# A depthwise conv and an ELU MLP on one core: two conv taps move from TensorE to VectorE, and the last piece of x is loaded early

## The chip, the cores and the metric

The kernel runs on one core of a Trainium2 chip. The metric is the device time in microseconds of one execution, here as the median of several. TensorE, VectorE (DVE), ScalarE (ACT), GpSimd (POOL) and the sync engine (SP) each run their own instruction stream in order, and wait for each other through semaphores.

## The reference

The input x is 8 x 4096 tokens of 192 values, that is 32768 rows. Each of 8 heads has 24 of the 192 columns and 7 weights. The weights go through a softmax, and each head's columns are convolved along the sequence with them (causally, zeros before the sequence). Then follow a matmul to 2048 columns, an ELU, and a matmul back to 192.

```python
w = np.exp(w - max(w)); w = w / (sum(w) + 1e-09)          # (8 heads, 7 taps)
out = np.einsum('hk,bskhg->bshg', w, x_unf)                # conv along s, 24 columns per head
h = out.reshape(B * S, D) @ w_in                           # (32768, 192) @ (192, 2048)
g = np.where(h > 0.0, h, np.exp(np.minimum(h, 0.0)) - 1.0)
return g @ w_out                                           # (2048, 192)
```

## The kernel before

The 32768 tokens are cut into 32 tiles of 1024 tokens (`NS`, index s). One half of a tile lies on partitions 0 to 63 of the h matmuls' operands and the other on 64 to 127, so two matmuls of 64 rows run side by side on TensorE. For each tile and each of 16 blocks of 128 hidden columns (`n` counts these blocks over all tiles, 512 in all) and each half, one *unit* runs: three h matmuls (L962) add up a 128x512 block of h in a PSUM bank; ScalarE makes exp(h) (L727); GpSimd clamps it to at most 1 (L684); VectorE makes max(exp - 1, h) and writes it as `gT` (L823), which frees the bank; the o matmuls (L985) use `gT` and `w_out`. There are eight PSUM banks. ScalarE also copies the conv's result (L723) and the outputs (L737) out of PSUM.

The order of TensorE's matmuls is written by a planner in the kernel's head (`pe_order`). It is a fixed list: every engine follows its own part of it, whatever the times turn out to be. The planner's costs and lists are not touched by the change.

The conv of tiles 1 to 31 is a matmul with a band matrix. `wband` holds each head's 7 weights in a row of zeros; SP writes it to DRAM (`conv_band`) with a row pitch one larger than the row, and reads it back as `Tm`, so that the weights lie on diagonals. The windows of x for it come by GpSimd's own DMAs (`load_x`, L600), which convert fp32 to bf16 on the way, two per tile. The last tile's second half has its fifth window, 70 rows, in a DMA of its own, because a full window would reach past the end of x. Their places in GpSimd's stream are in `x_before`.

The conv of tile 0 does not wait for the band. x is loaded as fp32 (`xs`), cast by ScalarE (`xb`), transposed by TensorE (`t` items, L884 and L895), and copied to `xT`, one 512-column row for each of three chunks j of 64 channels in two halves. Then TensorE multiplies `xT`, shifted by the tap, with `taps`, diagonal matrices of the weights (`d` items, L911): 7 matmuls of 512 columns for chunks 0 and 1, and 14 of 256 columns for chunk 2. ScalarE and VectorE copy the sums to `att` (L718, L809, L811), and the first h matmuls start. Before that VectorE also makes `taps` (L785), and copies two column parts of `w_in` from partitions 0 to 63 to 64 to 127 (`upper_half`, L748); ScalarE copies a third at its place `COPY_AT` (L733), and an SP DMA the rest (L1024). GpSimd meanwhile issues all start-up loads of `w_in`, `w_out` and x.

`first_read` says how many of ScalarE's (`s_fa`) and VectorE's (`s_fd`) start-up copies must be done before a start-up bank has been read.

Of the kernel before, what the change touches and what calls it, by code (L numbers as in the profile page):

```python
# [38 lines left out]
WCOLS = ((0, 4 * FC), (4 * FC, 8 * FC), (8 * FC, 16 * FC))  # L39
WOUT = (0, 4, 8, 16)  # L40
HALO = 8
BW = P + CW
XI = SUP // P
MM_H, MM_O, MM_C = 216.0, 82.5, 102.5
AHEAD = 100.0
# [18 lines left out]
def bass_lightweight_conv__then__act_elu_kernel(  # L64
# [327 lines left out]
    def tt_count(n, r):  # L392
        return unit_at[n, r] + 1

    band = nc.dram_tensor("conv_band", (P, HEADS * BW + P), BF16).ap()

    with ExitStack() as stack:
        def sbuf(name, shape, dt):
            return stack.enter_context(nc.sbuf_tensor(name, shape, dt))
# [4 lines left out]
        def sema(name):  # L404
            return stack.enter_context(nc.semaphore(name))
# [23 lines left out]
        wsum = sbuf("wsum", [HEADS, 1], FP32)  # L429
        wrs = sbuf("wrs", [HEADS, 1], FP32)  # L430
        wn = sbuf("wn", [HEADS, KSIZE], BF16)
        wnb = sbuf("wnb", [HEADS, HEADS, KSIZE], BF16)
        owner = sbuf("owner", [HEADS, P], BF16)
        block8 = sbuf("block8", [HEADS, HEADS, KSIZE], BF16)
        wband = sbuf("wband", [P, HEADS, BW], BF16)
        zw = sbuf("zw", [P, GS], BF16)
        scr = sbuf("scr", [P, 2], FP32)
        H = psum("H", [P, NBANK, GS])
# [28 lines left out]
        s_wd = sema("s_wd")  # L467
        s_wa = sema("s_wa")
        s_band = sema("s_band")
        s_att = [sema(f"s_att{i}") for i in range(2)]  # L470
        s_od = sema("s_od")
        s_cswap = sema("s_cswap")
# [19 lines left out]
        for s in range(NS):  # L492
            z_count += s % SPB == 0 and s > 0
            z_need[s] = z_count
            for g in range(2):
                x_count[s % NXB][g] += 16 * (s > 0) + 16 * ((s, g) == (NS - 1, 1))
                x_need[s, g] = x_count[s % NXB][g]

        def conv_read(W, m):
# [3 lines left out]
        def att_need(s):  # L503
# [5 lines left out]
            ("t", 1): (1, 0),  # L509
            ("t", 2): (2, 0),  # L510
            ("t", 3): (0, 2),
            ("d", 0): (3, 0),
            ("d", 1): (0, 3),
            ("d", 2): (4, 4),
        }

        def first_evacuated(W, what):
# [67 lines left out]
        def _gpsimd(g: bass.BassGpSimd):  # L585
            W = Waits(g)

            def load_x(s, gr):
                b = s % NXB
                if s >= NXB:  # L590
                    W(s_cv, CU * (s - NXB))
                if s == NXB:
                    W(s_zw, 1)
                def windows(w0, w1, rows):
                    src = bass.AP(
                        tensor=x_flat.tensor,
                        offset=(s * SUP + gr * GS + w0 * CW - PAD) * D,
                        ap=[[D, rows], [CW * D, w1 - w0], [1, D]],
                    )
                    g.dma_start(  # L600
                        xg[0:rows, b, 2 * w0 + gr : 2 * w1 : 2, :], src
                    ).then_inc(s_x[b][gr], 16)

                if s == NS - 1 and gr == 1:
                    windows(0, NWIN - 1, P)
                elif gr == 2:
                    gr = 1
                    windows(NWIN - 1, NWIN, GS - CW * (NWIN - 1) + PAD)
                else:
                    windows(0, NWIN, P)  # L610

# [81 lines left out]
        @block.scalar  # L693
        def _scalar(a):
            W = Waits(a)
            a.dma_start(  # L696
                xs[:, :, :], x_flat[0:SUP, :].rearrange("(p i) d -> p i d", i=XI)
            ).then_inc(s_xs, 16)
            a.memzero(scr[:, 0:1]).then_inc(s_scr)  # L699
            W(s_scr, 1)  # L700
            a.activation(scr[:, 1:2], scr[:, 0:1], ACT.Exp)
            W(s_set, 2)
            a.activation(wex[:], wq2[:], ACT.Exp).then_inc(s_wex)
            W(s_xs, 16)
            for j in range(3):
                a.activation(  # L706
                    xb[:, j, :, :].rearrange("p i (h e) -> p (i h) e", e=8),
                    xs[:, :, :].rearrange("p i (h j e) -> p j (i h) e", j=3, e=8)[:, j],
                    ACT.Copy,
                ).then_inc(s_cast)  # L710
            for sem, count, ins in (
                (s_xt, 3, transposed(1)),
                (s_xt, 4, transposed(2)),
                (s_first, 1, first_att(0, 0, GS)),
                (s_first, 3, first_att(2, 0, GS // 2)),
            ):
                W(sem, count)
                a.activation(*ins, ACT.Copy).then_inc(s_fa)  # L718
            for item in act_order:
                if item[0] == "c":  # L720
                    m = item[1]
                    W(s_cv, m + 1 - CU)
                    a.activation(*conv_evac(W, m), ACT.Copy).then_inc(s_ce)  # L723
                elif item[0] == "h":
                    i = unit_at[item[1:]]
                    W(s_h, i + 1)
                    a.activation(  # L727
                        E[:, i % NE, :], H[:, bank_of[item], :], ACT.Exp
                    ).then_inc(s_exp)
                    if i == COPY_AT:  # L730
                        c0, c1 = WCOLS[2][0], FC * LATE_Q
                        W(s_w[2], 48)
                        a.activation(  # L733
                            w_in[HP:P, :, c0:c1], w_in[0:HP, :, c0:c1], ACT.Copy
                        ).then_inc(s_wa)
                else:
                    a.activation(*out_evac(W, *item[1:]), ACT.Copy).then_inc(s_oev[item[2]])  # L737
            evacuated_by(W, NK - 1, 1)
            out_group(a, NK - 1, 1)

        @block.vector
        def _vector(v):
            W = Waits(v)

            def upper_half(v, k):
                c0, c1 = WCOLS[k]
                W(s_w[k], 48)
                v.tensor_copy(w_in[HP:P, :, c0:c1], w_in[0:HP, :, c0:c1]).then_inc(s_wc)  # L748

            v.memset(zw[:], 0.0).then_inc(s_zw)  # L750
            v.memset(wband[:], 0.0).then_inc(s_wb)
# [43 lines left out]
                xh[:, :].rearrange("p (h j e) -> p j h e", j=3, e=8),  # L795
            ).then_inc(s_xz)
            v.tensor_copy(
                wband[:, :, P - KSIZE : P][:, :, ::-1],
                H[:, bank_of["d", 2], HP : HP + HEADS * KSIZE].rearrange(
                    "p (h k) -> p h k", h=HEADS  # L800
                ),
# [1 line left out]
            for at, j in enumerate((0, 3)):  # L803
                W(s_xt, at + 1)
                v.tensor_copy(*transposed(j)).then_inc(s_fd)
            upper_half(v, 0)
            upper_half(v, 1)
            W(s_first, 2)
            v.tensor_copy(*first_att(1, 0, GS)).then_inc(s_fd)  # L809
            W(s_first, 3)  # L810
            v.tensor_copy(*first_att(2, GS // 2, GS)).then_inc(s_fd)  # L811
# [21 lines left out]
        def _tensor(pe):  # L833
# [16 lines left out]
            for item in pe_order:  # L850
# [51 lines left out]
                    ins.then_inc(s_xt)  # L902
                elif item[0] == "d":
                    j = item[1]
                    W(s_tap, 2 if j == 2 else 1)
                    first_evacuated(W, ("t", j))
                    first_evacuated(W, ("t", 3))
                    for tap in range(KSIZE):
                        for part in range(2 if j == 2 else 1):
                            c0, c1 = (GS // 2 * part, GS // 2 * (part + 1)) if j == 2 else (0, GS)  # L910
                            ins = pe.matmul(  # L911
                                H[:, bank_of[item] + part, c0:c1],
                                taps[:, tap, :],
                                xT[:, j, HALO - PAD + tap + c0 : HALO - PAD + tap + c1],
                                start=(tap == 0),
                                stop=(tap == KSIZE - 1),
                            )
                    ins.then_inc(s_first)
                elif item[0] == "c":
# [25 lines left out]
                elif item[0] == "h":  # L945
                    _, n, r, j = item
                    s, q = divmod(n, NQ)
                    if j == 0:
                        part = next(k for k in range(3) if FC * q < WCOLS[k][1])
                        W(s_w[part], 48)  # L950
                        if r == 1 and part < 2:
                            W(s_wc, part + 1)
                        elif r == 1 and q < LATE_Q:
                            W(s_wa, 1)
                        elif r == 1:
                            W(s_wd, 16)
# [43 lines left out]
        def _sync(sy):  # L1000
# [6 lines left out]
            W(s_tap, 2)  # L1007
            sy.dma_start(
                bass.AP(
                    tensor=band.tensor,  # L1010
                    offset=0,
                    ap=[[HEADS * BW + P + 1, P], [1, HEADS * BW]],
                ),
                wband[:, :, :].rearrange("p h i -> p (h i)"),
            ).then_inc(s_band, 16)
# [50 lines left out]
```

## Time and profile before

| what | value |
|---|---|
| median of 8 runs | 726.39 us (725.79 to 726.97) |
| profiled execution | 726.58 us, span 724.4 us |
| granted TensorE clock | 0.999 |
| TensorE busy | 718.0 us (99%), 11851 matmuls |
| VectorE, ScalarE, GpSimd busy | 641.4, 677.5, 669.6 us |
| conv of tile 0 (L911) | 28 matmuls, 4.7 us busy |
| x loads on GpSimd (L600) | 63 issues, 899 ns each |

The span runs from the first to the last instruction; the execution's own time holds some 2 us more around it. A row such as `7.85 1.11 DVE L748 COPY ...` gives the start and length in us, the engine, the line and the instruction; a bracket at its end gives the idle time of the engine before it, and what ended that. The chain of waits is followed back from the last instruction: a step on it had nothing running beside it that ended later and was waited for.

### The profile page before, as it was taken

How to read it: one execution, taken by the hardware profiler on the slowest of the kernel's cores; microseconds unless marked ns; L12 is line 12 of the kernel's file. 1: busy time of each engine (PE TensorE's matmuls, PEld its weight loads, DVE VectorE, ACT ScalarE, POOL GpSimd, SP SyncE). 2: the span in 40 equal slices, each digit the busy share in tenths (PEclk: the TensorE clock that was granted, in tenths of full speed). 3: DMA queues.
4: the chain of work that ended last, by engine and by line, in shares of the span. 5: the costliest groups of instructions: out<-in, count | busy, mean ns of one | idle time of the engine just before them, and what ended most of it. 6: DMA issues, size and time to landing. Idle time of an engine off the chain costs nothing.

```text
span 724.4 us, 27608 instructions
## 1 busy us (share of the span) xinstructions
PE 718.0 (99%) x11851; PEld 679.6 (94%) x11851; DVE 641.4 (89%) x1043; ACT 677.5 (94%) x1287; POOL 669.6 (92%) x1115
## 2 busy tenths in 40 slices
PE   8999999999999999999999999999999999999997
PEld 4689999999999999999999999999999999998997
DVE  5998898998899988989888989988989988988994
ACT  5999999999999999999999999999999999999993
POOL 8999999999999999999999999999999999999893
PEclk9999999999999999999999999999999999999999
DMA  9655363554254563344553445652445553546212
GB/s 192 89 85 70 66 97 72 93 90 76 59 96 72 87 96 61 75 83 86 86 97 53 81 76 94 86 92 48 92 75 95 86 69 67 96 72 85 71 34 68
DMA packets 132715, 59.11 MB, mean 82 GB/s; under 512 B 98664, under 2 KB 132016, under 8 KB 132592
## 3 DMA queue, kind: packets, MB, share of 16 engines
q1 hardware_dynamic: 88144, 39.57, 23.9%
q0 software_dynamic: 44032, 16.79, 23.0%
q8 instruction: 93, 1.52, 0.9%
q10 hardware_dynamic: 416, 0.98, 0.4%
q14 instruction: 30, 0.25, 0.1%
HBM read 34.83 MB, written 25.66 MB: 83 GB/s over the span
## 4 chain that ended last, share of the span: by engine, by line
PE 94%; POOL 2%; ACT 2%; DVE 1%; issue 0%; ACTq 0%; DVEq 0%
PE H L985 53%; PE H L962 37%; PE H L933 3%; POOL E L684 2%; DVE gT L823 1%; ACT E L727 1%; PE H L911 1%; POOL xg L600 0%; ACT csb L723 0%; PE H L858 0%; PE H L884 0%; ACT L699 0%; ACT osb L737 0%; DVE osb L814 0%; ACTq L696 0%
## 5 line engine op out<-in xcount | busy, mean ns | idle before, releaser
L823 DVE SCALAR_TENSOR_TENSOR gT<-E,H 128x512 f16<-128x512 f32 x1024 | 632.9, 683 | 67.3 <-POOL E L684 65.7
L985 PE MATMUL H<-w_out,gT 64*128 64x192 f16 x8192 | 682.5, 243 | 0.1
L962 PE MATMUL H<-att,w_in 64*128 64x512 bf16 x3072 | 681.1, 376 | 0.4 <-DVE gT L823 0.2
L985 PEld LDWEIGHTS H<-w_out,gT 64*128 64x128 f16 x8192 | 625.9, 94 | 21.7 <-PE H L985 1.3
L684 POOL TENSOR_SCALAR E<-E 128x512 f32<-128x512 f32 x1024 | 606.6, 612 | 42.1 <-ACT E L727 30.4
L727 ACT ACTIVATE E<-H 128x512 f32<-128x512 f32 x1024 | 593.2, 601 | 28.3 <-PE H L962 2.6
L962 PEld LDWEIGHTS H<-att,w_in 64*128 64x128 bf16 x3072 | 275.0, 93 | 8.0 <-issue 1.1
L933 PE MATMUL H<-xg,Tm 64*112 64x240 bf16 x496 | 92.6, 266 | 0.8 <-issue 0.6
L723 ACT ACTIVATE csb<-H 112x480 bf16<-112x480 f32 x124 | 70.0, 565 | 0.3
L737 ACT ACTIVATE osb<-H 128x384 f32<-128x384 f32 x127 | 61.6, 486 | 7.5 <-PE H L985 7.4
L933 PEld LDWEIGHTS H<-xg,Tm 64*112 64x112 bf16 x496 | 57.2, 125 | 4.3 <-DVE gT L823 1.1
L600 POOL DMA_DIRECT2D xg<-in_x_dram x63 | 56.3, 899 | 0.2 <-issue 0.2
L814 DVE COPY osb<-H 128x384 f32<-128x384 f32 x1 | 0.6, 558 | 7.3 <-PE H L985 7.3
L858 PE MATMUL H<-zw 128*128 128x512 bf16 x10 | 4.6, 629 | 1.2 <-DVE zw L750 1.2
L620 POOL DMA_DIRECT2D w_in<-in_moe_w_in_dram x9 | 5.2, 639 | 0.0
L911 PE MATMUL H<-xT,taps 128*128 128x512 bf16 (+1 forms) x28 | 4.7, 326 | 0.0
L911 PEld LDWEIGHTS H<-xT,taps 128*128 128x128 bf16 x28 | 2.6, 97 | 1.9
L718 ACT ACTIVATE att<-H 128x512 bf16<-128x512 f32 (+1 forms) x2 | 1.0, 490 | 3.4 <-PE H L911 3.4
L706 ACT ACTIVATE xb<-xs 128x512 bf16<-128x512 f32 x3 | 1.7, 619 | 2.5 <-DMA xs<-in_x_dram 2.5
L858 PEld LDWEIGHTS H<-zw 128*128 128x128 bf16 x10 | 1.2, 135 | 2.9 <-issue 1.6
L748 DVE COPY w_in<-w_in 64x1536 bf16<-64x1536 bf16 x2 | 2.3, 1126 | 1.4 <-DMA w_in<-in_moe_w_in_dram 1.3
L631 POOL DMA_DIRECT2D w_out<-in_moe_w_out_dram x3 | 2.7, 953 | 0.0
(39 smaller groups left out, 17.6 us busy)
## 6 DMA issues: line engine op xcount, KB each, us to landing
out_dram<-osb SPq DMA_DIRECT2D x127, 192.0 KB, 3.6
xg<-in_x_dram POOLq DMA_DIRECT2D x61, 240.0 KB, 5.1
xs<-in_x_dram ACTq DMA_DIRECT2D x1, 768.0 KB, 4.7
att<-csb SPq DMA_TRANSPOSE x31, 4.6
conv_band<-wband SPq DMA_DIRECT2D x1, 480.0 KB, 4.6
Tm<-conv_band SPq DMA_DIRECT2D x1, 448.0 KB, 7.6
w_in<-in_moe_w_in_dram POOLq DMA_DIRECT2D x6, 64.0 KB, 3.1
w_in<-in_moe_w_in_dram POOLq DMA_DIRECT2D x3, 128.0 KB, 5.2
```

What stands on the lines that cost most here:

```text
L600: g.dma_start(xg[0:rows, b, 2 * w0 + gr : 2 * w1 : 2, :], src).then_inc(s_x[b][gr], 16)
L620: g.dma_start(w_in[0:HP, j, c0:c1], bass.AP(tensor=moe_w_in.tensor, offset=8 * j * FF + c0, ap=[[CPH * FF, HEADS], [FF, 8], [1, c1 - c0]], ...
L684: g.tensor_scalar(out=E[:, i % NE, :], in0=E[:, i % NE, :], scalar1=1.0, scalar2=0.0, op0=ALU.min, op1=ALU.max,).then_inc(s_clp)
L723: a.activation(*conv_evac(W, m), ACT.Copy).then_inc(s_ce)
L727: a.activation(E[:, i % NE, :], H[:, bank_of[item], :], ACT.Exp).then_inc(s_exp)
L737: a.activation(*out_evac(W, *item[1:]), ACT.Copy).then_inc(s_oev[item[2]])
L823: v.scalar_tensor_tensor(out=gT[:, s % NG3, q, u, :], in0=E[:, i % NE, :], scalar=1.0, in1=H[:, bank_of[item], :], op0=ALU.subtract, op1=A ...
L858: pe.matmul(H[:, bank, :], zw[:, 0:P], zw[:, 0:GS], start=True, stop=True)
L911: ins = pe.matmul(H[:, bank_of[item] + part, c0:c1], taps[:, tap, :], xT[:, j, HALO - PAD + tap + c0 : HALO - PAD + tap + c1], start=(tap ...
L933: ins = pe.matmul(H[0:CW, bank_of["c", m], 256 * q : 256 * q + UC], Tm[rows, h, 0:CW], xg[rows, s % NXB, :, CPH * h : CPH * (h + 1)].rearr ...
L962: ins = pe.matmul(H[:, bank_of[item[:3]], :], w_in[HP * r : HP * (r + 1), j, FC * q : FC * (q + 1)], att[HP * r : HP * (r + 1), s % 2, j, ...
L985: ins = pe.matmul(acc_of(k, g)[:, D * kb : D * (kb + 1)], gT[HP * rt : HP * (rt + 1), t % NG3, q, g, t0 : t0 + P], w_out[HP * rt : HP * (r ...
```

## The change

For tile 0, chunks 0 and 1, TensorE makes only the first five taps. VectorE makes the other two, as a multiply and a multiply-add from `xT` into an fp32 buffer `part`, and the copy of the sum to `att` becomes an addition of `part`. Chunk 2 keeps its seven taps. The weights per partition are copied from PSUM to `wcol` first, and `taps` is built from that. The first `w_in` column part is now copied by ScalarE between its start-up copies, and the second by VectorE behind them. ScalarE no longer copies chunk 0, VectorE does both chunks.

Each head's row of the band is 128 wide instead of 240, with one more row of zeros behind the last head.

The last 70 rows of x are loaded as fp32 into `xl` by an SP DMA in the start-up, behind the read of `Tm`. Where GpSimd issued the separate DMA for the last tile, it now casts `xl` into `xg`, and TensorE's conv of the last tile waits for that (`s_xc`).

```diff
-BW = P + CW
+BW = P
+ON_DVE = (2, 2, 0)
+XL = GS - CW * (NWIN - 1) + PAD
...
-    band = nc.dram_tensor("conv_band", (P, HEADS * BW + P), BF16).ap()
+    band = nc.dram_tensor("conv_band", (P, (HEADS + 2) * BW), BF16).ap()
...
+        wcol = sbuf("wcol", [P, KSIZE], FP32)
+        part = sbuf("part", [P, 2, GS], FP32)
+        xl = sbuf("xl", [XL, D], FP32)
...
-            ("d", 0): (3, 0),
-            ("d", 1): (0, 3),
-            ("d", 2): (4, 4),
+            ("d", 0): (0, 3),
+            ("d", 1): (0, 4),
+            ("d", 2): (3, 5),
...
                 elif gr == 2:
-                    gr = 1
-                    windows(NWIN - 1, NWIN, GS - CW * (NWIN - 1) + PAD)
+                    W(s_xl, 16)
+                    g.tensor_copy(xg[0:XL, b, 2 * NWIN - 1, :], xl[:, :]).then_inc(s_xc)
...
-            for sem, count, ins in (
-                (s_xt, 3, transposed(1)),
-                (s_xt, 4, transposed(2)),
-                (s_first, 1, first_att(0, 0, GS)),
-                (s_first, 3, first_att(2, 0, GS // 2)),
-            ):
-                W(sem, count)
-                a.activation(*ins, ACT.Copy).then_inc(s_fa)
+            def upper_half(c0, c1):
+                a.activation(
+                    w_in[HP:P, :, c0:c1], w_in[0:HP, :, c0:c1], ACT.Copy
+                ).then_inc(s_wa)
+
+            for j in range(1, 3):
+                W(s_xt, j + 2)
+                a.activation(*transposed(j), ACT.Copy).then_inc(s_fa)
+            W(s_w[0], 48)
+            upper_half(*WCOLS[0])
+            W(s_first, 3)
+            a.activation(*first_att(2, 0, GS // 2), ACT.Copy).then_inc(s_fa)
...
+            v.tensor_copy(wcol[:], H[:, bank_of["d", 2], 0:KSIZE]).then_inc(s_tap)
+            W(s_tap, 1)
             v.tensor_tensor(
                 taps[:],
                 ident[:, :].unsqueeze(1).to_broadcast([P, KSIZE, P]),
-                H[:, bank_of["d", 2], 0:KSIZE].unsqueeze(2).to_broadcast([P, KSIZE, P]),
+                wcol[:, :].unsqueeze(2).to_broadcast([P, KSIZE, P]),
                 ALU.mult,
             ).then_inc(s_tap)
...
-            upper_half(v, 0)
-            upper_half(v, 1)
-            W(s_first, 2)
-            v.tensor_copy(*first_att(1, 0, GS)).then_inc(s_fd)
+            W(s_fd, 2)
+            for i in range(ON_DVE[0]):
+                for j in range(2):
+                    tap = KSIZE - 1 - i
+                    src = xT[:, j, HALO - PAD + tap : HALO - PAD + tap + GS]
+                    w = wcol[:, tap : tap + 1]
+                    if i == 0:
+                        W(s_fa, j)
+                        ins = v.tensor_scalar(
+                            out=part[:, j, :], in0=src, scalar1=w, scalar2=None, op0=ALU.mult
+                        )
+                    else:
+                        W(s_part, 2 * i + j - 1)
+                        ins = v.scalar_tensor_tensor(
+                            out=part[:, j, :],
+                            in0=src,
+                            scalar=w,
+                            in1=part[:, j, :],
+                            op0=ALU.mult,
+                            op1=ALU.add,
+                        )
+                    ins.then_inc(s_part)
+            for j in range(2):
+                W(s_part, 2 * ON_DVE[j] - 1 + j)
+                W(s_first, j + 1)
+                to, at = first_att(j, 0, GS)
+                v.tensor_tensor(to, at, part[:, j, :], ALU.add).then_inc(s_fd)
             W(s_first, 3)
             v.tensor_copy(*first_att(2, GS // 2, GS)).then_inc(s_fd)
+            c0, c1 = WCOLS[1]
+            W(s_w[1], 48)
+            v.tensor_copy(w_in[HP:P, :, c0:c1], w_in[0:HP, :, c0:c1]).then_inc(s_wc)
...
-                    for tap in range(KSIZE):
+                    last = KSIZE - 1 - ON_DVE[j]
+                    for tap in range(last + 1):
...
+                    if s == NS - 1:
+                        W(s_xc, 1)
...
-                Tm[:, :, :].rearrange("p h i -> p (h i)")[:, 0 : HEADS * BW - P],
-                band[:, P - 1 : HEADS * BW - 1],
+                Tm[:, :, :].rearrange("p h i -> p (h i)"),
+                band[:, P - 1 : P - 1 + HEADS * BW],
             ).then_inc(s_band, 16)
+            sy.dma_start(xl[:, :], x_flat[NT - XL : NT, :]).then_inc(s_xl, 16)
```

More of the change, by code (lines that the diff above doesn't have):

```diff
@@ L434, in bass_lightweight_conv__then__act_elu_kernel @@
         block8 = sbuf("block8", [HEADS, HEADS, KSIZE], BF16)
-        wband = sbuf("wband", [P, HEADS, BW], BF16)
+        wband = sbuf("wband", [P, HEADS + 1, BW], BF16)
         zw = sbuf("zw", [P, GS], BF16)
@@ L469, in bass_lightweight_conv__then__act_elu_kernel @@
         s_band = sema("s_band")
+        s_part = sema("s_part")
+        s_xl = sema("s_xl")
+        s_xc = sema("s_xc")
         s_att = [sema(f"s_att{i}") for i in range(2)]
@@ L495, in bass_lightweight_conv__then__act_elu_kernel @@
             for g in range(2):
-                x_count[s % NXB][g] += 16 * (s > 0) + 16 * ((s, g) == (NS - 1, 1))
+                x_count[s % NXB][g] += 16 * (s > 0)
                 x_need[s, g] = x_count[s % NXB][g]
@@ L730, in _scalar @@
                     if i == COPY_AT:
-                        c0, c1 = WCOLS[2][0], FC * LATE_Q
                         W(s_w[2], 48)
-                        a.activation(
-                            w_in[HP:P, :, c0:c1], w_in[0:HP, :, c0:c1], ACT.Copy
-                        ).then_inc(s_wa)
+                        upper_half(WCOLS[2][0], FC * LATE_Q)
                 else:
@@ L743, in _vector @@
             W = Waits(v)
[L745 to L748, printed above, removed]
             v.memset(zw[:], 0.0).then_inc(s_zw)
@@ L797, in _vector @@
             v.tensor_copy(
-                wband[:, :, P - KSIZE : P][:, :, ::-1],
+                wband[:, 0:HEADS, P - KSIZE : P][:, :, ::-1],
                 H[:, bank_of["d", 2], HP : HP + HEADS * KSIZE].rearrange(
@@ L904, in _tensor @@
                     j = item[1]
-                    W(s_tap, 2 if j == 2 else 1)
+                    W(s_tap, 3 if j == 2 else 2)
                     first_evacuated(W, ("t", j))
                     first_evacuated(W, ("t", 3))
-                    for tap in range(KSIZE):
-                        for part in range(2 if j == 2 else 1):
-                            c0, c1 = (GS // 2 * part, GS // 2 * (part + 1)) if j == 2 else (0, GS)
+                    last = KSIZE - 1 - ON_DVE[j]
+                    for tap in range(last + 1):
+                        for half in range(2 if j == 2 else 1):
+                            c0, c1 = (GS // 2 * half, GS // 2 * (half + 1)) if j == 2 else (0, GS)
                             ins = pe.matmul(
-                                H[:, bank_of[item] + part, c0:c1],
+                                H[:, bank_of[item] + half, c0:c1],
                                 taps[:, tap, :],
@@ L915, in _tensor @@
                                 start=(tap == 0),
-                                stop=(tap == KSIZE - 1),
+                                stop=(tap == last),
                             )
@@ L950, in _tensor @@
                         W(s_w[part], 48)
[L951 to L956, printed above, removed]
+                        if r == 1:
+                            W(*((s_wa, 1), (s_wc, 1), (s_wa, 2))[part] if q < LATE_Q else (s_wd, 16))
                         if s:
@@ L1006, in _sync @@
             sy.dma_start(xh[:, :], x_flat[GS - HALO : GS, :]).then_inc(s_xh, 16)
-            W(s_tap, 2)
+            W(s_tap, 3)
             sy.dma_start(
@@ L1011, in _sync @@
                     offset=0,
-                    ap=[[HEADS * BW + P + 1, P], [1, HEADS * BW]],
+                    ap=[[(HEADS + 2) * BW + 1, P], [1, (HEADS + 1) * BW]],
                 ),
```

## The prediction

> **What bounds the kernel now.** I read the page first, then the chain of waits in the two places that the edits touch (the first 14 us and the stretch around the last conv), and then the timelines of single engines there. The page's chain is on TensorE for nearly the whole span:
>
> ```profile
> PE 94%; POOL 2%; ACT 2%; DVE 1%; issue 0%; ACTq 0%; DVEq 0%
> ```
>
> So a change pays where TensorE has instructions removed, or waits removed, and nowhere else. The chain of the start-up (start, length, what) shows the first: the 28 conv matmuls of the first tile stand in the chain with nothing beside them, and the first h matmuls follow directly.
>
> ```profile
> 7.16 1.01 PE H L884 x32
> 8.16 4.68 PE H L911 x28
> 12.85 0.54 PE H L962 x4
> ...
> 13.45 0.42 PE H L962 x2
> 13.88 0.60 ACT E L727
> ```
>
> The timelines of the same stretch show what VectorE, ScalarE and GpSimd do beside those matmuls (start, length, instruction, and in brackets the idle time before it and who ended it):
>
> ```profile
> 7.04 0.78 DVE L805 CAST xT<-H 128x512 bf16<-128x512 f32 x2 [1.15 <-PE H L884]
> 7.85 1.11 DVE L748 COPY w_in<-w_in 64x1536 bf16<-64x1536 bf16 x1
> 10.29 1.14 DVE L748 COPY w_in<-w_in 64x1536 bf16<-64x1536 bf16 x1 [1.32 <-DMA w_in<-in_moe_w_in_dram]
> 11.46 0.69 DVE L809 CAST att<-H 128x512 bf16<-128x512 f32 x1
> 12.88 0.42 DVE L811 CAST att<-H 128x256 bf16<-128x256 f32 x1 [0.73 <-PE H L911]
> ...
> 17.42 0.84 ACT L733 ACTIVATE w_in<-w_in 64x768 bf16<-64x768 bf16 x1
> ...
> 11.64 1.86 POOL L600 DMA_DIRECT2D xg<-in_x_dram  x2
> 14.56 4.06 POOL L684 TENSOR_SCALAR E<-E 128x512 f32<-128x512 f32 x7 [1.06 <-ACT E L727]
> ```
>
> The second place is the only TensorE gap near 1 us after the start-up. It sits before the first conv of the last tile. GpSimd issued the last piece of x at 660.30, the DMA list gives 5.6 us to its landing, the sum is 665.9, and that is when the conv starts:
>
> ```profile
> 660.30 0.59 POOL L600 DMA_DIRECT2D xg<-in_x_dram  x1
> 664.96 0.38 PE L962 MATMUL H<-att,w_in 64*128 64x512 bf16 x1
> 665.93 0.12 PEld L933 LDWEIGHTS H<-xg,Tm 64*112 64x112 bf16 x1 [0.96 <-issue]
> 665.96 0.28 PE L933 MATMUL H<-xg,Tm 64*112 64x240 bf16 x1 [0.63 <-issue]
> ...
> xg<-in_x_dram POOLq DMA_DIRECT2D x1, 26.2 KB, 5.6
> ```
>
> The view calls the wait "issue", because no instruction ends it; its end coincides with the landing, so I read it as that transfer.
>
> **The change, part by part.**
>
> *Fewer taps on TensorE.* 14 matmuls of 512 columns and 14 of 256 are worth 21 wide ones, so one wide one takes 4.68 / 21 = 0.223 us. Two taps of two chunks leave: 4 x 0.223 = 0.89 us off the chain, provided that VectorE delivers in time.
>
> *Does VectorE deliver?* It is free at 7.85, when the two casts at L805 end. The removed L748 copy stood there. Now come two multiplies, two multiply-adds and two adds that read PSUM, and then the half copy of chunk 2. The nearest row for all of them is the 128x512 operation of the main loop (L823: 632.9 us for 1024, so 0.618 apart; 0.683 alone); the adds read PSUM just as it does. Six at 0.618 are 3.71; each waits for an earlier one of VectorE's own by a semaphore, and such handovers cost 0.03 in the wex, wsum, wrs chain, say 0.2 in all: done at 11.76. The other inputs are early: ScalarE's cast of chunk 1 ends near 8.4, and chunks 0 and 1 leave TensorE after 5 and 10 matmuls, at 9.3 and 10.4. Chunk 2 is now finished at 12.88 - 0.89 = 11.99. VectorE has 0.23 us to spare, so the half copy, the third h matmul and the first exp all come 0.89 earlier.
>
> A rule bears on this. The Trainium skill, VectorE: DVE Perf Modes, section on the perf-mode tier table, gives a `tensor_scalar` with SBUF operands twice the rate of an ordinary one, a two-tensor operation with fp32 none, and says of the fixed part that it is about 150 cycles. By that the two multiplies take about (256 + 150) / 0.96 = 0.42 us (an estimate from the page), the chain ends near 11.3, and the spare time is 0.7. By the row it is 0.23. Both give the same time; I keep the row.
>
> *A rule against it.* The Trainium skill, SBUF — State Buffer, section "Who interferes with whom", says that a VectorE instruction in a two-port mode and GpSimd shut each other out for whole instructions, and that two SBUF inputs clash with a GpSimd instruction that reads SBUF. GpSimd issues DMAs without a pause until 11.64 + 1.86 = 13.50. The trace speaks mildly: the two L748 copies, also SBUF to SBUF, met the same GpSimd issues at 1.11 and 1.14 us, while an issue takes 0.93 there (1.86 for two) against 0.90 as a mean of all 63. So the row's price for the clash is 0 to 0.1 us per issue. The rule's price is a wait for a whole issue, up to 0.9 us for each of the four SBUF operations. I take the row, and keep the rule for the range.
>
> *Does the shift carry to the end?* After the first exp every engine waits for another engine's instruction, so all of it moves, unless a transfer that starts at a fixed time becomes late. The nearest are x of tile 1 (issued at 9.2, 10.6 to landing, so 19.8; its first conv goes from 21.67 to 20.78) and the second part of w_out (10.0 + 10.3 = 20.3; its first use goes from 22.02 to 21.13). Both keep 0.8 us, and fewer bytes compete with them.
>
> *GpSimd as the next to be late.* Its first clamp at 14.56 had waited 1.06 us for the exp; moved up by 0.89, the wait is 0.17. That is the whole cover: if the DMA issues end more than 0.17 us later, the gain is cut one for one. The number of long SBUF copies on VectorE beside these issues falls from two to one, with two short multiplies instead, so I expect no slip.
>
> *Moved copies of w_in.* The first goes to ScalarE. By L733 768 columns cost 0.84, by the 512-column row at L718 0.60, so 1536 cost 0.84 + 768 x 0.95 / 1000 = 1.57 us. ScalarE is free from 8.85 until chunk 2 ends at 11.99, so it is hidden with 1.5 us to spare; uncovered it would cost that 1.57. The second goes behind the half copy: 12.41 + 1.13 = 13.54, before the first gT operation, which comes at 15.20 - 0.89 = 14.31. The h matmuls that need it start at 16.04 - 0.89 = 15.15. Hidden.
>
> *The extra copy to `wcol` ahead of `taps`.* About 0.17 us by the 24-column cast at L805 and 0.03 of handover. `taps` then ends near 5.8, TensorE wants it at 8.16, and the casts that follow have 1.15 us of idle time. Hidden.
>
> *Smaller bands.* The memset shrinks from 960 to 576 words, ahead of VectorE's wait for the exp: hidden. The DRAM write falls from 480 KB to 288 KB and the read back from 448 to 256 KB. The read back is needed at 21.67 and is there by 10.57 + 7.6 = 18.2. Earlier is worth nothing; the later issue (0.2 us, behind `wcol`) costs nothing. SP gains one issue of 54 KB ahead of its wait for w_in at 12.92; it is over by then. I set these at 0, with 0.1 either way.
>
> *The last piece of x.* The transfer becomes a load at the start, 640 us ahead of need, and GpSimd casts it. TensorE's wait of 0.96 us goes. Its successor is the preceding x load, issued at 657.18; even with the same 5.6 us it is there at 662.8, over 2 us before 665. On GpSimd the 0.59 us of issue becomes a cast of 70 x 192 elements, whose row is not in the trace. Between the 0.20 of a 128x128 memset at L635 and the 0.61 of a 128x512 clamp at L684, 192 columns lie near 0.33. GpSimd runs without a pause from 650.4 to 666.4, and a PEld row shows 0.30 us of waiting for VectorE at 662.32 behind it; 0.26 us less on GpSimd gives back perhaps 0.1. Bounds: 0 to 0.25.
>
> **Sum.** -0.89 - 0.96 - 0.10 = -1.95 us. The profiled execution took 726.58 (span 724.4 and 2.2 around it), so 724.63 for it; it stands 0.19 over the median of 726.39. For the median: 726.39 - 1.95 = 724.44.
>
> **The rivals.**
>
> *GpSimd or VectorE caps the start-up.* If GpSimd's issues slip by 1.06 us, or VectorE ends 0.9 us late, the 0.89 is lost and only the tail pays: 726.39 - 1.06 = 725.3. For it: the cover is only 0.17 us on GpSimd and 0.23 on VectorE. Against it: the mild rows of the copies. Half of it gives 724.9.
>
> *The tail pays less.* GpSimd is already behind at 662, so TensorE without its pause could run into VectorE's results instead. Between 662.4 and 665.0 the h pairs come about 0.635 us apart, GpSimd's clamps 0.614, so the lag should shrink. If half of the wait comes back: 724.9.
>
> *Slower: the shared port.* If each of the four SBUF operations of VectorE waits for a whole GpSimd issue of 0.9 us, its chain ends at 11.76 + 3.6 = 15.36 instead of 11.99 at the latest: 3.37 late against gains of 1.95, so 726.39 + 1.42 = 727.8. It decides from 2.2 us of such waiting (0.23 spare and 1.95 of gains). The 1.11 us copies speak against it.
>
> *The change doesn't do what it says:* the wait at 665 might not be that transfer's. Then only 0.89 + 0.1 come: 725.4. The landing time fits to 0.1 us, so this is unlikely.
>
> **How the numbers follow.** Both gains: 0.63, at 724.44 (own range 724.1 to 724.8). Start-up capped, wholly or half: 0.17, 724.9 to 725.4. Tail smaller or not that wait: 0.12, 724.9 to 725.4. Shared port: 0.06, 726.4 to 727.8. The rest, 0.02, no change. With 0.2 us for the run, 724.0 to 725.6 holds over 8 in 10. The bound of 0.2%, about what a measurement of this kernel can tell from no change, is 1.45 us: faster means under 724.94. That holds 0.61 of the first case and about a third of the next two: 0.70. Slower is the port case in its dear half and some of the rest: 0.06. The rest is 0.24.
>
> **What would show it.** L911 with 24 matmuls and 3.8 us in the chain; first exp near 12.99 and first clamp near 13.67; VectorE idle before its half copy. No idle row before the conv at 664; a 70x192 GpSimd row of about 0.3. Wrong: a first exp later than 13.2, VectorE multiplies over 0.8 us each, GpSimd issues that end past 13.7, or a new wait of TensorE for VectorE after 662.

## The result, and the profile after

The changed kernel took 724.2 us (median of 11 runs), the kernel before 726.56 (median of 32 runs beside it): a ratio of 0.9965, 95% interval 0.9957 to 0.9973, or 2.5 us less (2.0 to 3.1). The forecast was 724.44. The profiled execution took 723.88 us with a span of 721.9, against 726.58 and 724.4.

The profile's chain by engine is as it was, TensorE nearly everywhere:

```profile
PE 95%; POOL 2%; DVE 1%; ACT 1%; issue 0%; DVEq 0%; POOLq 0%
```

What differs stands at its two ends. In the start-up, the chain of waits of the changed kernel no longer runs over the conv matmuls. It runs over GpSimd's DMA issues until the first clamp, without a gap (start, length, what):

```profile
10.25 1.64 POOL w_out L639 x2
11.88 1.71 POOL xg L608 x2
13.59 0.67 POOL E L692
14.29 0.70 DVE gT L855
```

The timelines of single engines show why (start, length, what, idle time before). TensorE first, its transposes and the conv of tile 0, now 24 matmuls:

```profile
6.19 0.67 PE L916 MATMUL H<-ident,xb 64*64 64x64 bf16 x16
7.97 3.88 PE L944 MATMUL H<-xT,taps 128*128 128x512 bf16 x24
```

VectorE, with the four operations on SBUF, the two additions, and the half copy of chunk 2, for which it waits 0.62 us:

```profile
7.73 1.02 DVE L820 TENSOR_SCALAR part<-xT,wcol 128x512 f32<-128x512 bf16 x2
8.67 1.40 DVE L825 SCALAR_TENSOR_TENSOR part<-xT,wcol,part 128x512 f32<-128x512 bf16 x2
9.99 1.28 DVE L838 TENSOR_TENSOR att<-H,part 128x512 bf16<-128x512 f32 x2
11.89 0.42 DVE L840 CAST att<-H 128x256 bf16<-128x256 f32 x1 [0.62 <-PE H L944]
```

GpSimd, with its last start-up issues, the first clamp right behind them, and the cast of the last piece of x near the end:

```profile
11.84 1.75 POOL L608 DMA_DIRECT2D xg<-in_x_dram  x2
13.57 4.10 POOL L692 TENSOR_SCALAR E<-E 128x512 f32<-128x512 f32 x7
...
658.98 0.33 POOL L616 CAST xg<-xl 70x192 bf16<-70x192 f32 x1
```

From the first conv matmul to the first h matmul it is 11.78 - 7.97 = 3.81 us, where it was 12.78 - 8.10 = 4.68: 0.87 us less. The first exp starts at 12.87 and ends at 13.46, and GpSimd's issues end at 13.59, where the first clamp begins: exp and issues end almost together now.

At the other end, the list of waits between 640 and 690 us has no row of TensorE left; before, it had 0.96 us for x and 0.30 for VectorE. First the row of the kernel before for VectorE, then the whole list of the changed kernel (total us, times, longest):

```profile
662.32 0.09 PEld L985 LDWEIGHTS H<-w_out,gT 64*128 64x128 f16 x1 [0.30 <-DVE gT L823]
...
POOL E L692 <- ACT E L739: 3.6, 13, 0.3
DVE gT L855 <- POOL E L692: 3.3, 11, 0.7
```

I followed the difference of the two traces matmul by matmul. The lead of the changed kernel is 0.13 us at its first conv matmul, 1.00 at the first h matmul, and 1.02 at 36 us. It grows evenly to 1.31 by 650 us, then by 0.24 at 662 us and by 0.95 around the first conv of the last tile. The end has 2.49.

### The profile page after: what moved, and what is told of

Read it like the earlier page. It is cut to its first block, busy times and chain, and to the rows that moved or that the text cites. A ratio compares the mean times of both kernels' runs of the same rounds, so it can differ in the third digit from the quotient of the medians.

```text
span 721.9 us, 27609 instructions
## 1 busy us (share of the span) xinstructions
PE 716.0 (99%) x11847; PEld 677.6 (94%) x11847; DVE 642.8 (89%) x1048; ACT 677.9 (94%) x1287; POOL 669.4 (93%) x1115
## 4 chain that ended last, share of the span: by engine, by line
PE 95%; POOL 2%; DVE 1%; ACT 1%; issue 0%; DVEq 0%; POOLq 0%
PE H L1016 54%; PE H L993 38%; PE H L968 3%; DVE gT L855 1%; POOL w_in L628 1%; ACT E L739 1%; POOL xg L608 0%; POOL w_out L639 0%; ACT csb L735 0%; POOL E L692 0%; POOL owner L656 0%; DVE osb L846 0%; ACT osb L746 0%; POOL block L666 0%; POOL ident L645 0%
## 5 line engine op out<-in xcount | busy, mean ns | idle before, releaser
L944 PE MATMUL H<-xT,taps 128*128 128x256 bf16 (+1 forms) x24 | 3.9, 317 | 0.0
L720 ACT ACTIVATE w_in<-w_in 64x1536 bf16<-64x1536 bf16 (+1 forms) x2 | 2.3, 1162 | 0.0
```

Source lines behind the costliest of these rows:

```text
L944: ins = pe.matmul(H[:, bank_of[item] + half, c0:c1], taps[:, tap, :], xT[:, j, HALO - PAD + tap + c0 : HALO - PAD + tap + c1], start=(tap ...
```

## The experiments

Times are ratios to the kernel before, measured beside it in the same job; 0.001 is 0.73 us. "Lead" is how much earlier a matmul starts in the profile than in the profile of the kernel before. In experiments 5, 10, 11 and 12 the record of the first conv matmul is missing from the trace; its start is set 0.217 us, the usual distance, before the second's.

**1. The last piece of x alone** (`tail`). The xl parts of the diff, put into the kernel before.

```diff
+            W(s_xl, 16)
+            g.tensor_copy(xg[0:XL, b, 2 * NWIN - 1, :], xl[:, :]).then_inc(s_xc)
```

> The kernel before, with the last piece of x loaded early and cast by GpSimd, and nothing else changed. Theory A (the wait for the transfer and GpSimd's shorter step both count): no idle row before the first conv of the last tile, a GpSimd cast of 0.33 us, and 1.17 us less (0.94 for the wait, 0.23 for GpSimd): about 725.4 against 726.56. Theory B (the wait only moves, TensorE then waits for VectorE): under 0.5 us less. The start-up stays as before: first exp at 13.86.

Measured: 0.998 (0.9972 to 0.9989), 1.5 us less (0.8 to 2.0). The lead is 0.18 us from the start-up to 650 us, then grows by 0.24 at 662 and by 0.95 at the last tile's conv. The cast took 0.33 us. This is theory A; the rival of a wait that only moves (under 0.5 us) is out.

**2. The taps alone** (`taps`). The changed kernel with the band and the last piece as before; the cut shows only the band's width, all lines for band and `xl` are taken back with it.

```diff
-BW = P
+BW = P + CW
```

> The changed kernel with the old 240-wide band and the old late DMA for the last piece of x: only the taps on VectorE and the moves of the two w_in copies remain. Theory A (four matmuls fewer are the whole start-up gain): L911's successor has 24 matmuls in 3.8 us, the first exp comes 0.87 us earlier than 13.86, and the time falls by 0.9 us. Theory B (part of the 1.00 us by which the first h matmul came earlier is owed to the smaller band): 0.13 us less than that. The wait of 0.96 us before the last tile's conv is there again.

Measured: 0.998 (0.9971 to 0.9989), 1.6 us less (0.8 to 2.1); the expected 0.9 lies inside the interval, but the profile adds up in another way. The first h matmul leads by 0.97, of which 0.87 lie between the first conv matmul and it: theory A for the taps. But by 27 us only 0.27 are left. VectorE's half copy came 0.14 us late, which cost 0.12 at the first exp (13.01, a lead of 0.85), and then TensorE waited 0.55 us for w_out. VectorE's multiplies (first row), TensorE's timeline (second), and the chain of waits (third, start and length) show this:

```profile
7.75 1.86 DVE L817 TENSOR_SCALAR part<-xT,wcol 128x512 f32<-128x512 bf16 x2
...
21.80 0.24 PE L1011 MATMUL H<-w_out,gT 64*128 64x192 f16 x1 [0.55 <-DMA w_out<-in_moe_w_out_dram]
...
10.03 11.64 DMA w_out<-in_moe_w_out_dram
```

The second part of w_out was issued at 10.03 and landed at 21.67; its first use in the changed kernel is at about 21. And at the end, the separate DMA of x was issued at 659.98 and landed after 3.7 us instead of 5.6. TensorE did not wait for it in this profile, though nothing was changed in that part.

**3. The band alone** (`band`).

```diff
-BW = P + CW
+BW = P
```

> The kernel before with the 128-wide band rows alone. Theory A (band off the path): conv_band and Tm land earlier by up to 1 us, first h matmul and first exp within 0.05 us of 12.78 and 13.86 apart from scatter of the first load of x, and the time is the same within 0.2 us. Theory B (the shorter memset or the fewer bytes bring the first load of x, 0.2 us earlier in the changed kernel, and with it the start-up forward): the first cast at 5.34 instead of 5.54 and 0.13 us less.

Measured: 0.9997 (0.9988 to 1.0006): no difference, as theory A says. The lead of 0.30 us arises before the first conv matmul, which starts 0.30 earlier, and stays. It is not the band's: TensorE came to its full speed earlier in this execution. Its last four `zw` matmuls, which only keep it busy until x is there, show it, in the kernel before (first row) and here (second):

```profile
4.39 1.89 PE L858 MATMUL H<-zw 128*128 128x512 bf16 x4
...
4.40 1.14 PE L858 MATMUL H<-zw 128*128 128x512 bf16 x4
```

In the kernel before, these matmuls start 0.427 us apart; here the last ones start 0.217 apart. The section on the hardware has this for all runs. w_out's second part landed at 20.24.

**4. The late DMA, issued earlier** (`early_issue`).

```diff
-  x_before.setdefault(h_before(("c", CU * s + u + 1)), []).append((NS - 1, 2))
+  x_before.setdefault(h_before(("c", CU * s + u)), []).append((NS - 1, 2))
```

> The kernel before, with the separate DMA for the last piece of x issued right behind the issue before it (at about 658 us) instead of some 2.5 us later; it remains a GpSimd DMA of 0.59 us. Theory A (two terms): the wait before the last conv goes, 0.94 us less, while the wait of TensorE for VectorE at 662 stays (0.23 us not gained): about 725.6. Theory B (GpSimd's time is what counts, the transfer is a coincidence): no change. Theory C (landing is later because of the queue): a wait of some tenths is left before the conv.

Measured: 0.999 (0.9981 to 0.9998), 0.7 us less. The piece landed at 661.71, the wait before the last conv is gone, and the time fell, though its interval ends just under 1: theory B, no change, is out by the profile. GpSimd's two issues stand together, and TensorE waits for VectorE behind them (GpSimd's row, then the weight load's):

```profile
656.82 1.36 POOL L600 DMA_DIRECT2D xg<-in_x_dram  x2
...
659.61 0.09 PEld L962 LDWEIGHTS H<-att,w_in 64*128 64x128 bf16 x1 [0.31 <-DVE gT L823]
```

The lead falls by 0.48 us there, gets 0.24 back at 662, and gains 0.94 at the last conv: 0.70 in all, against 1.19 with the cast.

**5. The late DMA between two loads** (`tail_mid`).

```diff
-  x_before.setdefault(h_before(("c", CU * s + u + 1)), []).append((NS - 1, 2))
+  x_before.setdefault(h_before(("c", CU * s + u)) - 5, []).append((NS - 1, 2))
```

> The kernel before, with the separate DMA for the last piece of x moved five units ahead of the issue before it, so that it stands between two loads, at about 653.5 us. It remains a GpSimd DMA of 0.59 us. Theory A (the wait for the transfer counts 0.94 us, and three GpSimd steps close together count 0.2 to 0.5 us because they make VectorE late): no wait before the last conv and none for VectorE near 660, so about 1.1 us less than the kernel before, as with the cast. Theory B (a GpSimd step of 0.59 us costs TensorE the same wherever it stands): a wait for VectorE of 0.3 us or more is left, and the gain is 0.7 us as with the issue right behind.

Measured: 0.9992 (0.9983 to 1.0001). Counted from 650 us on, the lead grows by 0.71, the same as in 4. Theory A falls: distance to the neighbouring loads doesn't help, and the 0.6 us of GpSimd's time cost TensorE what they cost in 4, spread over several short waits. GpSimd's row, one of those waits, and TensorE's first transposes in this execution:

```profile
654.41 0.60 POOL L600 DMA_DIRECT2D xg<-in_x_dram  x1
...
656.45 0.09 PEld L962 LDWEIGHTS H<-att,w_in 64*128 64x128 bf16 x1 [0.20 <-DVE gT L823]
...
6.21 1.06 PE L884 MATMUL H<-ident,xb 64*64 64x64 bf16 x16
```

The timed interval, 0.1 us more to 1.2 less, holds both theories, so this rests on the profile. The last row is why this execution as a whole gained less than 0.71: the first 16 transposes took 1.06 us instead of 0.78, because TensorE was still at half speed, and the first conv matmul came 0.28 us later than in the kernel before.

**6. The changed kernel again** (`after_again`).

> The changed kernel once more, beside the runs that follow it: 0.9965 of the kernel before, and a second profile of it. Theory A (the extra 0.13 us in the start-up is scatter of the first load of x; the slow growth of the lead from 1.0 to 1.3 us between 20 and 660 us is a clock difference between two executions): the first load lands anywhere between 5.3 and 5.6, and the slow growth differs from the first profile's. Theory B (both belong to the change): the same as in the first profile.

Measured: 0.9964 (0.9952 to 0.9977). The first load of x landed at 5.49 us, where it was 5.32 in the first profile and 5.51 in the kernel before. Yet the first conv matmul leads by 0.17. So the load is not the cause, against theory A. The transposes are (0.63 us for 16), which began at 6.19 in both profiles: in the first one x was there earlier, but TensorE was still busy with its `zw` matmuls at half speed (their row, from 4.38, lasts to 6.27). The time at which it comes to full speed (5.75 us here, 6.32 in the first profile, 6.56 in the kernel before) is scatter, and no part of the change. The lead between 36 and 650 us goes from 1.05 to 1.08 only, so the even growth in the first profile belongs to that execution, as theory A says.

**7 and 8. More work for GpSimd in the start-up** (`after_2issues`, `before_2issues`).

```diff
+            for k in range(2):
+                g.dma_start(xd[:, k, :], x_flat[NT - 70 : NT, :]).then_inc(s_xd, 16)
             for i, (n, u) in enumerate(units):
```

> The changed kernel with two more GpSimd DMA issues (70 rows each into an unused tile, about 0.59 us each) behind the start-up's loads. Theory A (GpSimd's issues now end just when the first exp does, 13.55 against 13.47, so no cover is left): the first clamp moves from 13.57 to about 14.7, and the time grows by 1.1 us over the changed kernel. Theory B (the pipeline behind has slack enough): under 0.3 us.

> The kernel before with the same two more GpSimd issues. Theory A (its first clamp had waited 1.06 us for the exp, which covers them): the first clamp moves from 14.56 to 14.7, and the time grows by 0.1 us at most. Theory B (the added issues cost by something else, for instance their transfers): as much as in the changed kernel, about 1.1 us.

Measured: 0.9997 (0.9987 to 1.0007) for the changed kernel, 2.4 us over 0.9964, and 1.0006 (0.9997 to 1.0015) for the kernel before, 0.4 us more (0.2 less to 1.1 more). In the changed kernel, the exp was done at 13.9 and the clamp had to wait for the issues:

```profile
13.60 1.13 POOL L688 DMA_DIRECT2D xd<-in_x_dram  x2
14.74 3.50 POOL L696 TENSOR_SCALAR E<-E 128x512 f32<-128x512 f32 x6
```

The first clamp is 1.17 us later than in the changed kernel. In the kernel before it moved from 14.56 to 14.60 only. So the profiles show theory A: the cover that the kernel before had is used up. The 0.4 us of the kernel before are not clear of noise; its profile lost 0.28 us near 21.9, where the first conv of tile 1 waited for the second half of its x (landed at 21.67), and was level with the kernel before up to there.

The size in the changed kernel is larger than the expected 1.1 us. Its timed runs fall in two groups. The six of 725.4 to 725.9 had a mean granted clock of 0.999 to 1.000 and are 1.4 us over the changed kernel. The five of 727.2 to 727.9 had one of 0.994 to 0.998: their extra 2.3 us go with a lower clock. None of them was profiled, so why it was lower, and whether the issues brought it about, stays open.

**9. A third tap** (`after_3taps`).

```diff
-ON_DVE = (2, 2, 0)
+ON_DVE = (3, 3, 0)
```

> The changed kernel with three taps of chunks 0 and 1 on VectorE instead of two, so two matmuls fewer. Theory A (VectorE had 0.62 us to spare, and two multiply-adds cost 1.32 us there): chunk 2 is done 0.43 us earlier on TensorE, but VectorE's half copy comes at about 12.6 instead of 11.89, so the first exp is 0.7 us later than 12.87 and the time grows by 0.7 us. Theory B (TensorE alone sets the start-up): the first exp 0.43 us earlier, capped by GpSimd's issues at 13.55, so no change of the time.

Measured: 0.9978 (0.9969 to 0.9987), 1.0 us more than the changed kernel by the ratios, whose intervals touch (0.8 by the medians). VectorE's four multiply-adds and ScalarE's first exp:

```profile
8.63 2.72 DVE L825 SCALAR_TENSOR_TENSOR part<-xT,wcol,part 128x512 f32<-128x512 bf16 x4
...
13.44 3.53 ACT L739 ACTIVATE E<-H 128x512 f32<-128x512 f32 x7 [1.75 <-PE H L993]
```

The exp starts at 13.44 instead of 12.87. Counted from the first conv matmul (7.82 and 7.97) it is 0.72 us later, where 0.7 was expected: theory A. VectorE is the bound here, so three taps are too many; one tap was not tried.

**10. Both start-up parts without the last piece** (`taps_band`). All `xl` parts of the diff are taken back, and nothing else; the cut shows one of them.

```diff
-                    W(s_xl, 16)
-                    g.tensor_copy(xg[0:XL, b, 2 * NWIN - 1, :], xl[:, :]).then_inc(s_xc)
+                    gr = 1
+                    windows(NWIN - 1, NWIN, GS - CW * (NWIN - 1) + PAD)
```

> The changed kernel with the old late DMA for the last piece of x: taps on VectorE, the moved w_in copies and the smaller band together. In the run with the taps alone TensorE waited 0.55 us for the second part of w_out, which landed at 21.67, and the start-up's lead of 0.97 us fell to 0.27. Theory A (the old band's bytes hold that transfer up): with the smaller band it lands before 20.6, no such wait, and the lead at 26 us and later is 1.0 us. Theory B (that run was an unlucky landing): the lead differs by chance, and w_out lands anywhere between 20.2 and 21.7. The end has the wait for the last piece again, unless it lands in under 4.7 us.

Measured: 0.9981 (0.9972 to 0.9989). w_out landed at 20.55, no wait for it. The lead is 0.79 at the first h matmul (0.87 from the first conv matmul, which came 0.08 late) and 0.80 at 45 us. So far theory A. The separate x landed after 4.0 us, so TensorE did not wait for it in this profile either.

**11. More bytes** (`after_morebytes`).

```diff
+            sy.dma_start(band2[:, :], wband[:, :, :].rearrange("p h i -> p (h i)")).then_inc(s_mb, 16)
```

> The changed kernel with 288 KB more written from SBUF to an unused DRAM tensor, issued by SP right behind the band's write. Theory A (bytes on the DMA engines in the first 20 us decide when w_out's second part lands, and the start-up's gain hangs on it): it lands at 21.2 or later instead of 20.2, TensorE waits for it by 0.2 to 0.7 us near 21 us, and the lead over the kernel before falls from 1.0 to 0.3 to 0.7 us; about 0.5 us more time than the changed kernel. Theory B (the landing doesn't hang on those bytes): it lands at 20.2 to 20.4 and the time stays.

Measured: 0.997 (0.9958 to 0.9981), not apart from the changed kernel. w_out landed at 20.82, half a microsecond later, but in time: counted from the first conv matmul, the lead is 0.87 at the first h matmul and 0.90 at 45 us. The direction is that of theory A, the size is not: theory A wanted 21.2 or later. 288 KB more from SBUF to DRAM do less than the old band's 192 KB more each way; why is not shown.

**12. The old band in the changed kernel** (`after_oldband`).

```diff
-BW = P
+BW = P + CW
```

> The changed kernel with the old 240-wide band rows, all else kept. In six profiles with the old band w_out's second part landed at 20.3 to 22.2, in six with the new one at 20.1 to 20.6. Theory A (the start-up's gain hangs on that landing): it lands at 21 or later, TensorE waits for it by 0.2 to 0.7 us near 21.5, and at 26 us and later the lead, counted from the first conv matmul of tile 0, is 0.2 to 0.7 us instead of 0.87; the time lies 0.2 to 0.7 us over the changed kernel's 0.9964. Theory B (the wait in the run with the taps alone was bad luck): no such wait and the full lead.

Measured: 0.9975 (0.9964 to 0.9986); the interval overlaps that of the changed kernel. w_out landed at 21.03, and the second half of x for tile 1 at 20.54, and the first conv of tile 1 waited. The view names no engine for this wait; it ends 0.21 us behind that landing, as in the kernel before with two more issues (21.67 and 21.88), so I read it as that transfer:

```profile
20.75 0.12 PEld L968 LDWEIGHTS H<-xg,Tm 64*112 64x112 bf16 x1 [0.33 <-issue]
```

The lead counted from the first conv matmul is 0.87 us at the first h matmul and 0.69 at 45 us: 0.18 lost. TensorE did not wait for w_out itself. So the old band delays the landings, as theory A says, and with the taps on VectorE the delay cost 0.55 us in one profile (experiment 2, for w_out) and 0.18 in the other (for x). In the timed ratios this is too small to be seen.

Over all profiles, w_out's second part landed at 20.31, 21.32, 21.67, 21.17, 22.23, 21.72 and 21.03 with the old band (the kernel before, experiments 1, 2, 4, 8, 5, 12), and at 20.20, 20.27, 20.24, 20.32, 20.07 and 20.55 with the new one (the changed kernel twice, 3, 7, 9, 10), or 20.82 with the extra bytes. That is 1.1 us on the mean. The need in the changed kernel is at about 21.1: all those with the new band came before it, and five of the seven with the old one after it.

## Why the prediction was right

Both parts that the prediction counted on are real, each shown alone (experiments 1 and 2). The three terms of its sum, 1.95 us, came to 0.87 + 0.95 + 0.24 = 2.06 in the profiles.

**Fewer taps.** 0.89 was predicted; 0.87 came, in both profiles of the changed kernel and with the taps alone. In both profiles of the changed kernel the shift carried to the end, as argued; with the taps alone it did not.

**VectorE.** The chain of six operations was predicted to end at 11.76 by the row of L823, and near 11.3 by the page on perf modes (the Trainium skill, VectorE: DVE Perf Modes, "The perf-mode tier table"); it ended at 11.27. The two multiplies took 0.47 us each from start to start, near the 0.42 estimated from the page, so the row was the wrong choice, without harm. (The page has twice the ordinary rate in its column for fp32, and four times in that for bf16; it has no row for bf16 in and fp32 out, as here.)

In other runs the two multiplies together took 1.10 to 1.86 us, and single ones 0.91 to 0.99 in experiments 2, 7, 10 and 11. "VectorE multiplies over 0.8 us each" was one of the prediction's signs of being wrong, so a part of the shared-port rival was there; with the taps alone it made VectorE 0.14 us late. Its full price, a wait of 0.9 us for each of four operations, did not appear. The rule of the Trainium skill that the prediction cites (SBUF — State Buffer, "Who interferes with whom") fits. In the two profiles with multiplies of 0.49 us, GpSimd's next issue began at 8.51 and 8.47; with the slowest multiplies (0.99 and 0.95, 0.80 and 0.95) it began at 8.32 and 8.35. What one engine gains there, the other seems to lose in part. This was not tested by itself.

**GpSimd's cover.** Predicted 0.17 us left; it was 0: the issues ended at 13.59 instead of 13.50, the exp came 0.12 earlier than forecast, and the first clamp started right behind the issues. Experiments 7 and 8 show that this is a bound now. The rival in which it eats the gain was close, but cost nothing; that it just fitted was partly luck.

**Bands at 0.** Alone they are worth 0 (experiment 3). The weak step is the check of landings: "Both keep 0.8 us" rested on 20.3 for w_out, from one profile, the earliest of seven with the old band; the others show up to 22.2. With the need at 21.1, the smaller band is what brought that transfer in time. It was set at 0, and without it TensorE waited 0.55 us in experiment 2 and lost 0.18 in experiment 12. The sum came right because the change as a whole has the smaller band.

**The last piece.** 0.96 + 0.10 was predicted; 0.95 + 0.24 came, in both profiles of the changed kernel and with this part alone. The cast's 0.33 us was right to the last digit. What 0.26 us of GpSimd are worth to TensorE was set too low, 0.10 instead of 0.24, near its upper bound of 0.25.

The wait itself is not in every execution of the old code. Of the five profiles with the late DMA at its old place, it landed after about 5.5 us in three (the kernel before, experiments 3 and 8) and after 3.7 to 4.0 in two (experiments 2 and 10), with no wait in those. That the profile behind the forecast was one of the three was luck. The packets in the traces show what differs. In the three, DMA packets of only 4 to 768 bytes took 1.3 to 1.6 us; they began 0.2 to 0.5 us behind the start of a 16 KB load on the instruction queue (at 662.70, 662.94 and 664.14), and the last packets of x came behind that standstill. In the two, that load started at 663.25 and 663.28, when the packets of x were through, and no other packet near it took over 0.7 us. Why the packets stand still is not shown, and nothing was run to test it.

So the terms don't add up in the timed medians: the last piece alone took off 1.5 us and the taps alone 1.6, but both with the band only 2.5. How much of the 2.5 is the wait is known from experiment 1 alone (0.8 to 2.0 us for both halves of the term).

**The rest.** The profiled execution gained 2.49: 0.87 + 0.24 + 0.95, 0.13 from TensorE's earlier full speed, and 0.29 of even growth that the second profile did not have. The last two are no part of the change. The timed gain, 2.0 to 3.1 us, holds the 2.06 at its lower edge; whether the 0.4 us between 2.06 and its middle are more than noise is open.

## What to carry to other kernels

A single late transfer can sit on the critical path of a kernel that is 99% busy: search the timeline of the bounding engine for its one gap, and load what it waits for early by a queue that has time. Before work is taken off the start-up's bounding engine, write down how long each neighbour has been waiting, because the second engine's wait is the most that can be gained; here GpSimd's 1.06 us allowed the 0.87 and no more, as its issues ended with the exp. And take the margin of a DMA landing from several profiles, not one: here the same transfer, with the old band, landed within a range of 1.9 us.

## What the runs showed of the hardware that was not expected

TensorE's first 16 transposes took 0.63 to 1.06 us from execution to execution, and the whole start-up moves by that. Their starts show two speeds: pair by pair they are 0.107 us apart in some executions and 0.056 in others, and the `zw` matmuls ahead of them 0.427 or 0.217. In each of the 14 traces the spacing halves where the trace's record of the full clock begins, and this is anywhere between 3.89 us (experiment 12) and 7.29 us (experiment 7) behind the start of the span. (The profile's windows print a clock of 1.00 before that too, where they have no record.) With the full clock before 6.1 us and x in time, the first conv matmul started at 7.80 to 7.93; with the full clock at 6.3 to 6.6 it started at 7.97 to 8.11, and with 7.2 to 7.3 at 8.38 to 8.40. No edit set this time, and a lead of 0.3 us in one profile says nothing about an edit until it is counted from behind this point. Experiment 10 started at 8.18 for another reason: its first load of x landed only at 5.73.

The same 26 KB DMA took 3.7 to 5.6 us from issue to landing at the same place of the program. A VectorE copy of 64x1536 elements from SBUF to SBUF beside GpSimd's DMA issues took 0.69 to 1.14 us.
